# Attention keys in three chunks of 128 and a block-diagonal one, sums on VectorE and casts on ScalarE

## The chip, the cores and the metric

One core of a Trainium2 chip. The metric is the device time of one execution in microseconds (us). Engines: TensorE (PE; its weight loads are PEld), VectorE (DVE), ScalarE (ACT), GpSimd (POOL) and SyncE (SP), which issues all DMAs here. TensorE's clock has two levels, 1.2 and 2.4 GHz; the profile gives the granted one as a share of the higher.

## The reference

Attention with 4 batches, 12 heads, 448 positions and 64 columns a head, then two dense blocks on the 1792 x 768 result:

```python
scores = matmul(q, k.T) / 8
scores = cap * tanh(scores / cap)                # cap = 30
attn = softmax(scores)
x = matmul(attn, v)          # 1792 x 768 after the heads are joined
h = x @ w_in1;  x = (h - tanh(h)) @ w_out1       # 768 -> 2048 -> 768
h = x @ w_in2;  x = (h * sigmoid(1.702 * h)) @ w_out2
```

All weights come as 64-bit floats.

## The kernel before, in words

**Numbers.** Products are made from float32r parts: a value is cast to a high part, and a subtract gives the low part (`hi_act`, `hi_dve`, `lo_dve`, `lo_pool`, L92 to L102). A product of two split values takes three matmuls: high x high, low x high, high x low.

**Attention.** Heads go in pairs, six pairs a batch, 24 in all; q and k of two heads lie side by side in 128 partitions. The 448 keys of a head are four chunks of 112 (`C = 4`, `CP = 112`). For each pair:

- `load_qk` (four DMAs) and `load_v` (one) fetch it; `prep` transposes q and k on TensorE, casts the high part on ScalarE and subtracts on VectorE, 896 columns each; `v_split` does the same for v.
- `qk` makes the scores of one chunk, transposed: 112 keys x 448 queries of both heads. The two heads use the upper and the lower half of TensorE's rows, so six matmuls run as three pairs.
- `softmax` does tanh and a shifted exponential on ScalarE (112 x 896), the high cast `ph` and the low subtract `pl` on VectorE, and adds the exponentials to the running sum `s` on GpSimd (L312). No maximum is taken.
- `pv` multiplies the chunk with v: per head two matmuls, whose output holds the product with v's high part in one half of the partitions and with its low part in the other.
- `split_sum` splits the sum on VectorE; `pair_out` sums over partitions with a matrix of ones (four matmuls), takes the reciprocal on VectorE, joins the two halves and multiplies.

**Order.** `attention` is a generator written out by hand: it walks over the chunks with scores two chunks ahead of `pv` (`PV_LAG = 2`) and yields after each step, nine times a pair. Batch 0's attention runs alone until its last pair is out (L557). From then on a loop (L571) walks through the matrix work of a batch matmul by matmul and takes a step of the next batch's attention whenever `ATT_RATES` says that one is owed; no step falls due in the first quarter of batch 0. The tile framework then orders each engine's instructions statically, by program order and by what it reckons to be ready, and sets the waits; an engine runs its list in that order.

**Matrix work.** Per batch four parts (`gemm_in`, `gemm_out`, twice) of 288 matmuls of 448 columns. Weights come in chunks, fetched and split two chunks ahead (`ahead`). In batch 0 each is converted from its 64-bit form (`w_convert`, ScalarE and VectorE), split with the low part on GpSimd, and kept in DRAM; later batches read it back.

**Buffers.** Exponentials `t_p` three, high and low probabilities `ph_p` three each (the sum's parts among them), two PSUM tiles `ps_b` for scores, transposes, sums and output, a third one while batch 0's attention runs, one for `pv`.

Of the kernel before, what the change touches and what calls it, by code (L numbers as in the profile page):

```python
# [34 lines left out]
PV_LAG = 2  # L35

# [8 lines left out]
def attention_moe_moe(ctx, tc, q, k, v, cap, w_in1, w_out1, w_in2, w_out2, out):  # L45
# [11 lines left out]

    nc = tc.nc
# [3 lines left out]
    C = 4  # L62
    CP = S // C
# [10 lines left out]
    raw_p = pool("raw", 2)  # L74
    rv_p = pool("rawv", 1)
# [33 lines left out]
    ones = const.tile([CP, 2, P], F32R, name="ones")  # L109
# [10 lines left out]
    first = ExitStack()  # L120
    vs_f = first.enter_context(tc.tile_pool(name="vs_f", bufs=1))
# [123 lines left out]
    def load_v(g):
        if g >= NG:
            return
        b, hp = divmod(g, NP)
        tv = rv_p.tile([CP, 2, C, D], F32, tag="rv", name="rv")
        nc.sync.dma_start(  # L250
            out=tv.rearrange("p h c d -> p h (c d)"),
            in_=v[b, 2 * hp:2 * hp + 2].rearrange("h (p c) d -> p h (c d)", c=C),
        )
        rawv[g] = tv

    def prep(g):
        t = raw.pop(g)
        ps = big_ps(g, "ps_qk")
        for i in range(2):
            for c in range(C):  # L260
                nc.tensor.transpose(
                    ps[:, i, c * CP:(c + 1) * CP], t[:, i, c, :], ident[:CP, :CP]
                )
        h = qk_p.tile([P, 2, S], F32R, tag="qkh", name="qkh")
        l = qk_p.tile([P, 2, S], F32R, tag="qkl", name="qkl")
        hi_act(h, ps[:, :, :S])
        lo_dve(l, ps[:, :, :S], h)
        qkt[g] = (h, l)

    def v_split(g):  # L270
        tv = rawv.pop(g)
        t = (vs_f if g < NP and g % 2 else vs_p).tile([CP, 2, C, P], F32R, tag="vs", name="vs")
        for j in range(2):
            hh, ll = t[:, j, :, j * D:(j + 1) * D], t[:, j, :, (1 - j) * D:(2 - j) * D]
            hi_act(hh, tv[:, j])
            lo_dve(ll, tv[:, j], hh)
# [4 lines left out]
    def qk(n):  # L281
        g, c = divmod(n, C)
        h, l = qkt[g]
        ps = big_ps(g, "ps_sc")
        for m, (kk, qq) in enumerate(((h, h), (l, h), (h, l))):
            for j in range(2):
                a = slice(j * D, (j + 1) * D)
                nc.tensor.matmul(  # L288
                    ps[:CP, j, :S], kk[a, 1, c * CP:(c + 1) * CP], qq[a, 0, :], start=(m == 0), stop=(m == 2)
                )  # L290
        sc_ps[n] = ps

    def softmax(n):
        g, c = divmod(n, C)
        ps = sc_ps.pop(n)
        t = t_p.tile([CP, 2, S], F32, tag="t", name="t")
        nc.scalar.activation(out=t, in_=ps[:CP, :, :S], func=AF.Tanh, scale=tsc[:CP])  # L297
        nc.scalar.activation(out=t, in_=t, func=AF.Exp, scale=cpos[:CP], bias=cshift[:CP])  # L298
        h = ph_p.tile([CP, 2, S], F32R, tag="ph", name="ph")
        l = ph_p.tile([CP, 2, S], F32R, tag="pl", name="pl")  # L300
        hi_dve(h, t)
        lo_dve(l, t, h)
        phl[n] = (h, l)
        if c == 0:
            pt[g] = t
            return
        if c == 1:
            sums[g] = s_p.tile([CP, 2, S], F32, tag="s", name="s")
            a = pt.pop(g)
        else:  # L310
            a = sums[g]
        nc.gpsimd.tensor_tensor(out=sums[g], in0=a, in1=t, op=ALU.add)  # L312

    def pv(n):
        g, c = divmod(n, C)
        h, l = phl.pop(n)
        if c == 0:
            pvs[g] = ps_v.tile([P, 2, 512], F32, tag="v", name="ps_pv")
        for j in range(2):
            for m, pp in enumerate((h, l)):  # L320
                nc.tensor.matmul(  # L321
                    pvs[g][:, j, :S], vsp[g][:, j, c, :], pp[:, j, :],
                    start=(c == 0 and m == 0), stop=(c == C - 1 and m == 1),
                )

    def split_sum(g):
        s = sums.pop(g)
        h = ph_p.tile([CP, 2, S], F32R, tag="ph", name="sh")
        l = ph_p.tile([CP, 2, S], F32R, tag="pl", name="sl")
        hi_dve(h, s)  # L330
# [290 lines left out]
```

## Time and profile before

| | us |
|---|---|
| median of 3 runs (lowest, highest) | 1409.39 (1408.37, 1414.51) |
| profiled execution | 1408.85 |
| its span, first to last instruction | 1406.8 |
| busy: TensorE, VectorE, ScalarE, GpSimd | 1253.5, 1087.6, 822.2, 506.9 |

Batch 0's attention alone lasts until 150.7 us of the span, batch 0's matrix work until 555.5, batch 1's until 869, batch 2's until 1164.5. Busy time of TensorE is modelled from pipelined matmuls, so the distance from start to start is the better price of one.

### The profile page before, as it was taken

To read this page: it belongs to the slowest core of one execution; us is meant where nothing else is said; L and a number is where in the kernel's file an instruction comes from. 1 tells how busy PE (TensorE), PEld (TensorE's weight loads), DVE (VectorE), ACT (ScalarE), POOL (GpSimd) and SP (SyncE) were. 2 spreads that over 40 slices of the span, in tenths; PEclk is the share of its full clock that TensorE was granted. 3 is DMA by queue.
4 is the path that set the end of the run, shared out by engine and by line. 5 is a ranking of instruction groups with operands and counts; after the bars stand their busy time and mean duration, and the time that the engine had idled before them with its cause. 6 is when DMAs were issued, how large, how long until landed. Compare 5 with 4: busy or idle time off the path is not lost.

```text
span 1406.8 us, 17148 instructions
## 1 busy us (share of the span) xinstructions
PE 1253.5 (89%) x5964; PEld 1060.2 (75%) x5964; DVE 1087.6 (77%) x1229; ACT 822.2 (58%) x1100; POOL 506.9 (36%) x274
## 2 busy tenths in 40 slices
PE   7677766887887869988999999999999999999998
PEld 3344655776666757776888788888888899999997
DVE  5999899898989988997677875997788766933432
ACT  5764687777776674874455544684455535733421
POOL 2444555655766453432124320431154212301300
PEclk6565999998898989999999999999999999999999
DMA  6233155777566655763323446734333347533332
GB/s 172 67 89 105 54 168 161 240 235 231 185 202 189 196 173 185 264 209 86 116 86 118 123 113 178 196 104 122 119 95 105 99 133 226 149 119 113 108 113 66
DMA packets 164550, 204.36 MB, mean 145 GB/s; under 512 B 53360, under 2 KB 121456, under 8 KB 164464
## 3 DMA queue, kind: packets, MB, share of 16 engines
q1 hardware_dynamic: 164464, 203.27, 47.6%
q8 instruction: 47, 0.77, 0.2%
q14 instruction: 39, 0.32, 0.1%
HBM read 157.45 MB, written 45.78 MB: 144 GB/s over the span
## 4 chain that ended last, share of the span: by engine, by line
PE 50%; DVE 8%; issue 3%; DMA 1%; ACT 1%; POOL 0%; SPq 0%; DVEq 0%; ACTq 0%; POOLq 0%
PE ps_y L486 26%; PE ps_h L466 18%; PE ps_pv L321 3%; PE ps_sc L288 2%; DVE wl L99 1%; DVE r L347 1%; DVE g_q L439 1%; DVE g_t L437 1%; DMA wr<-kept 1%; PE ps_o L509 1%; DVE pl L99 1%; DVE g_q L440 1%; DVE ph L96 1%; PE ps_sum L339 0%; DVE g_far L426 0%
## 5 line engine op out<-in xcount | busy, mean ns | idle before, releaser
L466 PE MATMUL ps_h<-xh,wh 128*128 128x448 f32 x768 | 290.5, 379 | 46.5 <-DVE g_far L426 31.7
L486 PE MATMUL ps_y<-gh,wh 128*128 128x448 f32 x768 | 288.1, 375 | 15.9 <-DVE gh L96 8.1
L99 DVE TENSOR_TENSOR wl<-wr,wh 128x768 fp32r<-128x768 f32 (+1 forms) x172 | 170.9, 996 | 160.9 <-ACT wh L93 67.2
L466 PE MATMUL ps_h<-xl,wh 128*128 128x448 f32 x768 | 287.7, 375 | 4.1 <-DVE xl L99 4.1
L93 ACT CAST wh<-wr 128x768 fp32r<-128x768 f32 (+1 forms) x195 | 153.3, 786 | 235.7 <-PE ps_y L486 156.2
L486 PE MATMUL ps_y<-gl,wh 128*128 128x448 f32 x768 | 289.2, 377 | 1.6 <-POOL gl L102 1.6
L466 PEld LDWEIGHTS ps_h<-xh,wh 128*128 128x128 f32 x768 | 147.9, 193 | 73.1 <-DVE g_far L426 40.6
L312 POOL TENSOR_TENSOR s<-s,t 112x896 f32<-112x896 f32 x48 | 123.6, 2575 | 190.6 <-ACT t L298 190.2
L486 PE MATMUL ps_y<-gh,wl 128*128 128x448 f32 x768 | 189.7, 375 | 0.0
L466 PE MATMUL ps_h<-xh,wl 128*128 128x448 f32 x768 | 184.4, 371 | 0.0
L102 POOL TENSOR_TENSOR wl<-wr,wh 128x768 fp32r<-128x768 f32 (+1 forms) x68 | 145.8, 2147 | 105.7 <-DVE wh L96 62.9
L486 PEld LDWEIGHTS ps_y<-gh,wh 128*128 128x128 f32 x768 | 147.4, 192 | 35.2 <-DVE gh L96 8.8
L466 PEld LDWEIGHTS ps_h<-xl,wh 128*128 128x128 f32 x768 | 147.9, 193 | 19.0 <-DVE xl L99 4.3
L102 POOL TENSOR_TENSOR gl<-g_q,gh 128x448 fp32r<-128x448 f32 x64 | 91.5, 1429 | 194.7 <-ACT gh L93 111.2
L486 PEld LDWEIGHTS ps_y<-gl,wh 128*128 128x128 f32 x768 | 147.3, 192 | 18.8 <-issue 4.1
L99 DVE TENSOR_TENSOR pl<-t,ph 112x896 fp32r<-112x896 f32 x96 | 157.9, 1644 | 2.1
L486 PEld LDWEIGHTS ps_y<-gh,wl 128*128 128x128 f32 x768 | 146.5, 192 | 16.8 <-issue 3.8
L466 PEld LDWEIGHTS ps_h<-xh,wl 128*128 128x128 f32 x768 | 145.2, 190 | 16.4 <-issue 4.2
L102 POOL TENSOR_TENSOR gl<-g_g,gh 128x448 fp32r<-128x448 f32 x64 | 92.0, 1439 | 175.2 <-ACT gh L93 115.3
L297 ACT ACTIVATE t<-ps_sc,tsc 112x896 f32<-112x896 f32 x96 | 96.4, 1006 | 84.5 <-PE ps_sc L288 77.8
L96 DVE CAST ph<-t 112x896 fp32r<-112x896 f32 x96 | 102.4, 1066 | 38.7 <-ACT t L298 26.8
L193 ACT ACTIVATE wd<-wd 128x768 uint16<-128x768 uint16 (+1 forms) x68 | 125.2, 1849 | 1.1
(73 smaller groups left out, 1868.8 us busy)
## 6 DMA issues: line engine op xcount, KB each, us to landing
wr<-kept SPq DMA_DIRECT2D x100, 384.0 KB, 3.1
wd<-in_moe_w_in_dram SPq DMA_DIRECT2D x64, 384.0 KB, 4.4
wr<-kept SPq DMA_DIRECT2D x72, 320.0 KB, 3.0
wd<-in_moe_w_out_dram SPq DMA_DIRECT2D x48, 384.0 KB, 4.2
kept<-wr SPq DMA_DIRECT2D x44, 384.0 KB, 5.0
wh<-kept_hl SPq DMA_DIRECT2D x32, 384.0 KB, 3.3
wl<-kept_hl SPq DMA_DIRECT2D x32, 384.0 KB, 3.8
kept<-wr SPq DMA_DIRECT2D x24, 320.0 KB, 4.9
```

The costliest lines, as they stand in the source:

```text
L93: nc.scalar.copy(out=dst, in_=src)
L96: nc.vector.tensor_copy(out=dst, in_=src)
L99: nc.vector.tensor_tensor(out=dst, in0=src, in1=hi.bitcast(F32), op=ALU.subtract)
L102: nc.gpsimd.tensor_tensor(out=dst, in0=src, in1=hi.bitcast(F32), op=ALU.subtract)
L193: nc.scalar.mul(out=half[:, :, :, 2], in_=half[:, :, :, 1], mul=F64_LOW)
L288: nc.tensor.matmul(ps[:CP, j, :S], kk[a, 1, c * CP:(c + 1) * CP], qq[a, 0, :], start=(m == 0), stop=(m == 2))
L297: nc.scalar.activation(out=t, in_=ps[:CP, :, :S], func=AF.Tanh, scale=tsc[:CP])
L312: nc.gpsimd.tensor_tensor(out=sums[g], in0=a, in1=t, op=ALU.add)
L321: nc.tensor.matmul(pvs[g][:, j, :S], vsp[g][:, j, c, :], pp[:, j, :], start=(c == 0 and m == 0), stop=(c == C - 1 and m == 1),)
L347: nc.vector.reciprocal(out=r, in_=ps[:, 0, :S])
L466: nc.tensor.matmul(ps[:, :S], w[:, kk, :], x[kk], start=(m == 0), stop=(m == len(seq) - 1))
L486: nc.tensor.matmul(ps[:, :S], w[:, f - f0, :], x[f], start=(c == 0 and m == 0), stop=(c == len(parts) - 1 and m == len(seq) - 1),)
```

## The change

Keys become three chunks of 128 (`C = 3`) and a rest of 64 keys a head (`T = 64`). The rests of the two heads share one chunk of 128 partitions: k's is laid out block-diagonally, zero elsewhere, and v's rest has zeros in the other head's partitions. So a pair has three chunks of 128 x 896 and one of 128 x 448, whose scores are three matmuls over all 128 rows. The zeros are set once, in fixed tiles for q, k and v, two of each (one for v after batch 0).

The high casts of the exponentials and of the sum go to ScalarE, the running sum to VectorE; it leaves the last chunk out, whose exponentials go straight into the matmuls with ones (six instead of four, with a third block of ones). q and k are cast and subtracted separately; v's cast and subtract are one instruction each. The reciprocal takes a buffer of `t_p`. The steps are written out: seven a pair. q and k of a pair are eight DMAs, v's four, the output's two.

```diff
-                last_raw[0] = nc.sync.dma_start(
-                    out=t[:, i, :, j * D:(j + 1) * D], in_=src[b, 2 * hp + j].rearrange("(p c) d -> p c d", c=C)
+                e = slice(j * D, (j + 1) * D)
+                h = src[b, 2 * hp + j]
+                nc.sync.dma_start(
+                    out=t[:, i, :C, e], in_=h[:C * P].rearrange("(p c) d -> p c d", c=C)
                 )
+                a = j * T * i
+                last_raw[0] = nc.sync.dma_start(out=t[a:a + T, i, C, e], in_=h[C * P:])
...
+            for c in range(C + 1):
+                n = P if c < C or i else T
+                nc.tensor.transpose(ps[:, i, c * P:c * P + n], t[:n, i, c, :], ident[:n, :n])
+        h = qk_p.tile([P, S + SK], F32R, tag="qkh", name="qkh")
+        l = qk_p.tile([P, S + SK], F32R, tag="qkl", name="qkl")
+        for a, z, x in ((0, S, ps[:, 0, :S]), (S, S + SK, ps[:, 1, :SK])):
+            hi_act(h[:, a:z], x)
+            lo_dve(l[:, a:z], x, h[:, a:z])
...
+        t = (vs_f if g < NP and g % 2 else vs_p).tile([P, 2, C + 1, P], F32R, tag="vs", name="vs")
+        hi_act(t[:, :, :, :D], tv)
+        lo_dve(t[:, :, :, D:], tv, t[:, :, :, :D])
...
-    def qk(n):
-        g, c = divmod(n, C)
+    def qk(g, c):
         h, l = qkt[g]
         ps = big_ps(g, "ps_sc")
+        k0 = S + c * P
         for m, (kk, qq) in enumerate(((h, h), (l, h), (h, l))):
+            if c == C:
+                nc.tensor.matmul(ps[:, 0, :S], kk[:, k0:k0 + P], qq[:, :S], start=(m == 0), stop=(m == 2))
+                continue
             for j in range(2):
                 a = slice(j * D, (j + 1) * D)
-                nc.tensor.matmul(
-                    ps[:CP, j, :S], kk[a, 1, c * CP:(c + 1) * CP], qq[a, 0, :], start=(m == 0), stop=(m == 2)
-                )
-        sc_ps[n] = ps
...
+                nc.tensor.matmul(ps[:, j, :S], kk[a, k0:k0 + P], qq[a, :S], start=(m == 0), stop=(m == 2))
...
-        hi_dve(h, t)
...
+        hi_act(h, t)
         lo_dve(l, t, h)
...
-        nc.gpsimd.tensor_tensor(out=sums[g], in0=a, in1=t, op=ALU.add)
...
+        elif c < C:
+            a = pt.pop(g) if c == 1 else sums[g]
+            if c == 1:
+                sums[g] = s_p.tile([P, 2, S], F32, tag="s", name="s")
+            nc.vector.tensor_tensor(out=sums[g], in0=a, in1=t, op=ALU.add)
...
-                    pvs[g][:, j, :S], vsp[g][:, j, c, :], pp[:, j, :],
-                    start=(c == 0 and m == 0), stop=(c == C - 1 and m == 1),
+                    pvs[g][:, j, :S], vsp[g][:, j, c, :], pp[:, j if c < C else 0, :],
+                    start=(c == 0 and m == 0), stop=(c == C and m == 1),
...
+        if c < C:
+            phl.pop((g, c))
...
-        hi_dve(h, s)
+        h = ph_p.tile([P, 2, S], F32R, tag="ph", name="sh")
+        l = ph_p.tile([P, 2, S], F32R, tag="pl", name="sl")
+        hi_act(h, s)
         lo_dve(l, s, h)
...
+        th, tl = phl.pop((g, C))
...
-        for m, (j, pp) in enumerate(((0, h), (0, l), (1, h), (1, l))):
-            nc.tensor.matmul(ps[:, 0, :S], ones[:, j, :], pp[:, j, :], start=(m == 0), stop=(m == 3))
+        seq = [(2, th[:, 0]), (2, tl[:, 0])] + [(j, pp[:, j]) for j in range(2) for pp in (h, l)]
+        for m, (j, pp) in enumerate(seq):
+            nc.tensor.matmul(ps[:, 0, :S], ones[:, j, :], pp, start=(m == 0), stop=(m == len(seq) - 1))
...
-        r = s_p.tile([P, S], F32, tag="r", name="r")
+        r = t_p.tile([P, S], F32, tag="t", name="r")
...
-        load_qk(0)
-        load_qk(1)
-        load_v(0)
         yield False
         prep(0)
         v_split(0)
+        load_qk(2)
         load_v(1)
         yield False
...
+        for g in range(NG + 1):
+            last = g > 0 and g % NP == 0
             if g < NG:
-                qk(n)
+                qk(g, 0)
+                qk(g, 1)
                 yield False
-                softmax(n)
-                if c == 0:
-                    load_qk(g + 2)
-                if c == 2 and g + 1 < NG:
-                    prep(g + 1)
-                    yield False
...
+                softmax(g, 0)
+            if g > 0:
+                pv(g - 1, 2)
+                split_sum(g - 1)
+                yield False
+                pv(g - 1, 3)
+                pair_out(g - 1)
+                yield last
+                if g >= NP and g < NG:
+                    v_split(g)
+                    load_v(g + 1)
+            if g == NG:
+                break
+            softmax(g, 1)
+            qk(g, 3)
+            qk(g, 2)
+            yield False
+            softmax(g, 3)
+            pv(g, 0)
+            yield False
+            softmax(g, 2)
+            if g + 1 < NG:
+                prep(g + 1)
+                load_qk(g + 3)
+                yield False
+                if g + 1 < NP:
                     v_split(g + 1)
                     load_v(g + 2)
...
+            pv(g, 1)
+            yield False
...
+        nc.tensor.transpose(ps[:T, C * P:], y[:, C * P:], ident)
+        nc.vector.tensor_copy(out=o[:, :C].rearrange("p c e -> p (c e)"), in_=ps[:, :C * P])
+        nc.scalar.copy(out=o[:T, C], in_=ps[:T, C * P:])
+        dst = out[b * S:(b + 1) * S, e * P:(e + 1) * P]
+        nc.sync.dma_start(out=dst[:C * P].rearrange("(p c) e -> p c e", c=C), in_=o[:, :C])
+        nc.sync.dma_start(out=dst[C * P:], in_=o[:T, C])
...
+    for t in raws_qk:
+        nc.vector.memset(t[:, 1, C], 0.0)
+    for t in raws_v:
+        nc.vector.memset(t[:, :, C], 0.0)
+    load_qk(0)
     nc.sync.dma_start(out=capr, in_=cap.partition_broadcast(P))
+    load_v(0)
+    load_qk(1)
...
-    per_batch = 9 * NP
+    per_batch = 7 * NP
```

## Rows read from the trace of the kernel before

**Rows 1.** Windows: start:end, length, busy us (instructions) by engine, granted clock, DMA share, GB/s
```profile
12.00:150.70 138.70, 95.40 (x331) 57.35 (x329) 125.90 (x125) 92.12 (x105) 60.83 (x24) 0.62 0.36 100
150.70:244.40 93.70, 67.55 (x293) 57.43 (x293) 89.64 (x102) 70.34 (x98) 49.05 (x28) 0.95 0.44 136
244.40:327.50 83.10, 74.02 (x342) 64.33 (x343) 73.55 (x80) 62.41 (x65) 46.32 (x23) 0.94 0.70 228
327.50:430.00 102.50, 82.88 (x370) 69.44 (x369) 90.27 (x90) 77.70 (x86) 68.65 (x35) 0.88 0.66 212
430.00:555.50 125.50, 100.29 (x477) 82.89 (x478) 112.83 (x112) 79.68 (x90) 62.32 (x29) 0.88 0.58 183
555.50:869.00 313.50, 295.46 (x1473) 252.74 (x1472) 248.19 (x287) 174.73 (x257) 89.75 (x50) 0.99 0.46 140
869.00:1164.50 295.50, 291.49 (x1477) 253.57 (x1476) 226.72 (x262) 160.85 (x239) 89.92 (x49) 1.00 0.44 128
```

**Rows 2.** Lines by shape, whole span: busy us, mean ns; idle before it and releaser
```profile
L99 DVE TENSOR_TENSOR pl<-t,ph 112x896 fp32r<-112x896 f32 x96 | 157.9, 1644 | 2.1
...
L312 POOL TENSOR_TENSOR s<-s,t 112x896 f32<-112x896 f32 x48 | 123.6, 2575 | 190.6 <-ACT t L298 190.2
L298 ACT ACTIVATE t<-t,cshift,cpos 112x896 f32<-112x896 f32 x96 | 108.6, 1133 | 1.5
...
L96 DVE CAST ph<-t 112x896 fp32r<-112x896 f32 x96 | 102.4, 1066 | 38.7 <-ACT t L298 26.8 <-PE ps_pv L321 11.1
...
L297 ACT ACTIVATE t<-ps_sc,tsc 112x896 f32<-112x896 f32 x96 | 96.4, 1006 | 84.5 <-PE ps_sc L288 77.8 <-issue 6.5
L93 ACT CAST wh<-wr 128x768 fp32r<-128x768 f32 x111 | 92.3, 832 | 117.7 <-PE ps_y L486 55.5 <-PE ps_h L466 42.4 <-DVE wr L195 12.1
...
L99 DVE TENSOR_TENSOR sl<-s,sh 112x896 fp32r<-112x896 f32 x24 | 26.0, 1084 | 0.8
...
L93 ACT CAST gh<-g_g 128x448 fp32r<-128x448 f32 x32 | 18.2, 569 | 39.0 <-DVE g_g L457 39.0
...
L99 DVE TENSOR_TENSOR xl<-xs,xh 128x448 fp32r<-128x448 f32 x24 | 15.1, 632 | 3.6 <-ACT xh L93 3.6
```

**Rows 3.** Instructions of the tile ph: shortest, median and longest ns, first and last start
```profile
L96 DVE CAST ph<-t x96: 600/627/4293, 18.8 to 1134.6; 112x896 fp32r<-112x896 f32 x96
L99 DVE TENSOR_TENSOR pl<-t,ph x96: 1020/1093/3016, 19.4 to 1135.3; 112x896 fp32r<-112x896 f32 x96
```

**Rows 4.** Timelines of GpSimd and VectorE: start, us; an add and a low subtract
```profile
83.11 2.33 POOL L312 TENSOR_TENSOR s<-t 112x896 f32<-112x896 f32 x1 [3.19 <-DVE sl L99]
...
83.93 2.46 DVE L99 TENSOR_TENSOR pl<-t,ph 112x896 fp32r<-112x896 f32 x1
```

**Rows 5.** Timeline of VectorE: start, us; first and last of batch 0's six reciprocals
```profile
40.74 2.94 DVE L347 RECIPROCAL r<-ps_sum 128x448 f32<-128x448 f32 x1
...
147.69 2.94 DVE L347 RECIPROCAL r<-ps_sum 128x448 f32<-128x448 f32 x1
```

**Rows 6.** Timeline of TensorE: two matmuls at the half level; a score group, two at full
```profile
91.24 0.57 PE L321 MATMUL ps_pv<-ph,vs 112*128 112x448 f32 x1
91.61 0.57 PE L321 MATMUL ps_pv<-pl,vs 112*128 112x448 f32 x1
...
958.75 0.46 PE L288 MATMUL ps_sc<-qkh 64*112 64x448 f32 x2
...
959.55 0.89 PE L486 MATMUL ps_y<-gh,wl 128*128 128x448 f32 x3
...
963.31 0.36 PE L321 MATMUL ps_pv<-ph,vs 112*128 112x448 f32 x1
963.51 0.37 PE L321 MATMUL ps_pv<-pl,vs 112*128 112x448 f32 x1
```

**Rows 7.** SyncE's queue: a timeline row of two issues; a row of its waits (us, times, longest)
```profile
1.18 1.38 SPq L240 DMA_DIRECT2D raw<-in_q_dram  x2
...
SPq L240 <- PE ps_qk L261: 28.9, 7, 7.0
```

More of the change, by code (lines that the diff above doesn't have):

```diff
@@ L33 @@
 ATT_END_0, ATT_END = 1.0, 0.97
-PV_LAG = 2
 EXP_TOP = 60.0
@@ L61, in attention_moe_moe @@
     P = 128
-    C = 4
-    CP = S // C
+    C = 3
+    T = S - C * P
+    SK = C * P + 2 * T
     NP = H // 2
@@ L108, in attention_moe_moe @@
     cshift = const.tile([P, 1], F32, name="cshift")
-    ones = const.tile([CP, 2, P], F32R, name="ones")
+    ones = const.tile([P, 3, P], F32R, name="ones")
+    raws_qk = [const.tile([P, 2, C + 1, 2 * D], F32, name=f"raw{i}") for i in range(2)]
+    raws_v = [const.tile([P, 2, C + 1, D], F32, name="rv0")]
     tsc = const.tile([P, 1], F32, name="tsc")
@@ L120, in attention_moe_moe @@
     first = ExitStack()
+    rv_f = first.enter_context(tc.tile_pool(name="rv_f", bufs=1))
+    raws_v.append(rv_f.tile([P, 2, C + 1, D], F32, name="rv1"))
     vs_f = first.enter_context(tc.tile_pool(name="vs_f", bufs=1))
@@ L248, in load_v @@
         b, hp = divmod(g, NP)
[L249 to L252, printed above, removed]
-        )
+        tv = raws_v[g % 2 if g < NP else 0]
+        for j in range(2):
+            h = v[b, 2 * hp + j]
+            nc.sync.dma_start(
+                out=tv[:, j, :C].rearrange("p c d -> p (c d)"), in_=h[:C * P].rearrange("(p c) d -> p (c d)", c=C)
+            )
+            nc.sync.dma_start(out=tv[j * T:(j + 1) * T, j, C], in_=h[C * P:])
         rawv[g] = tv
@@ L271, in v_split @@
         tv = rawv.pop(g)
[L272 to L276, printed above, removed]
+        t = (vs_f if g < NP and g % 2 else vs_p).tile([P, 2, C + 1, P], F32R, tag="vs", name="vs")
+        hi_act(t[:, :, :, :D], tv)
+        lo_dve(t[:, :, :, D:], tv, t[:, :, :, :D])
@@ L302, in softmax @@
+        sc_ps[g, c] = ps
+    def softmax(g, c):
+        ps = sc_ps.pop((g, c))
+        n = 1 if c == C else 2
+        t = t_p.tile([P, n, S], F32, tag="t", name="t")
+        nc.scalar.activation(out=t, in_=ps[:, :n, :S], func=AF.Tanh, scale=tsc)
+        nc.scalar.activation(out=t, in_=t, func=AF.Exp, scale=cpos, bias=cshift)
+        h = ph_p.tile([P, n, S], F32R, tag="ph", name="ph")
+        l = ph_p.tile([P, n, S], F32R, tag="pl", name="pl")
+        hi_act(h, t)
         lo_dve(l, t, h)
-        phl[n] = (h, l)
+        phl[g, c] = (h, l)
@@ L317, in pv @@
+    def pv(g, c):
+        h, l = phl[g, c]
         if c == 0:
@@ L545, in attention_moe_moe @@
     nc.vector.tensor_scalar(out=cshift, in0=cshift, scalar1=0.0, scalar2=None, op0=ALU.min)
-    for j in range(2):
-        nc.vector.tensor_scalar(
-            out=ones[:, j, j * D:(j + 1) * D], in0=ident[:CP, :D], scalar1=0.0, scalar2=1.0,
-            op0=ALU.mult, op1=ALU.add,
-        )
-        nc.vector.tensor_scalar(
-            out=ones[:, j, (1 - j) * D:(2 - j) * D], in0=ident[:CP, :D], scalar1=0.0, scalar2=None, op0=ALU.mult
-        )
+    for m in range(3):
+        for j in range(2):
+            a = slice(j * D, (j + 1) * D)
+            for z in range(2):
+                nc.vector.tensor_scalar(
+                    out=ones[z * T:(z + 1) * T, m, a], in0=ident[z * T:(z + 1) * T, :D], scalar1=0.0,
+                    scalar2=float(j == (z if m == 2 else m)), op0=ALU.mult, op1=ALU.add,
+                )
     nc.vector.reciprocal(out=tsc, in_=cpos)
```

60 lines of the change are left out of this document (6 added, 54 removed).

## The prediction

> **What bounds the kernel now.** I read the stages first, by the busy time of each engine in eight stretches of the span [rows 1]; the reader is to see which engine is nearly full in each. From 12 to 150.7 us attention of batch 0 runs alone: VectorE is busy 125.9 of 138.7 us, ScalarE 92.1, TensorE 95.4 at a mean granted clock of 0.62. The four stretches from 150.7 to 555.5 are batch 0's matrix work, the conversion of the weights and attention of batch 1: VectorE is again fullest, 89.6 of 93.7, then 73.6 of 83.1 (TensorE 74.0 there), 90.3 of 102.5, 112.8 of 125.5. From 555.5 on TensorE is the bound: 295.5 of 313.5, then 291.5 of 295.5 at full clock. So 543 us hang mostly on VectorE, and 851 on TensorE.
>
> Next, the groups of instructions by shape [rows 2], and the shortest and median instance of two of them [rows 3]. The high cast of a chunk's exponentials (ph) has a mean of 1066 ns but a median of 627 and a longest of 4293; the low subtract (pl) 1644 against 1093 and 3016. GpSimd's own adds last 2575 ns. One add runs from 83.11 to 85.44; a low subtract that starts at 83.93 ends at 86.39, 0.95 us after it [rows 4]. So VectorE does not only do the work, it waits behind GpSimd, and those waits count as busy.
>
> The Trainium skill, SBUF — State Buffer, section "SBUF: two separate sides", says that the port pair of VectorE and GpSimd is an exclusive lock: a VectorE instruction in a two-port mode, or with two SBUF inputs, is blocked for the whole of a GpSimd instruction that reads SBUF. The excess in the rows agrees in kind. By the rule alone, three adds a pair could cost up to 3 x 2.58 = 7.7 us of VectorE per pair; the rows' excess, (1066 - 627) x 4 + (1644 - 1093) x 4, is 4.0 us, and I use that.
>
> Then the reciprocals, one per pair: the first of batch 0 starts at 40.74 and the sixth at 147.69, so a pair takes 107/5 = 21.4 us there [rows 5]. Last TensorE's order of time [rows 6]: a single attention matmul takes 0.20 us at the full level and 0.37 at the half level (1.2 GHz); six score matmuls, run as three pairs, take 959.55 - 958.75 = 0.80 us, of which 3 x 0.20 is streaming and 0.20 is going from whole-height to half-height use and back.
>
> **VectorE, per pair.** Before: four ph, four pl, the sum's cast and its subtract: 4 x 1.066 + 4 x 1.644 + 0.63 (as a ph median) + 1.084 = 12.6 us. After: three full subtracts, one half one (as a 448-column subtract, 0.632), the sum's subtract and two adds, each as sl, which no GpSimd add disturbs: 3 x 1.084 + 0.63 + 1.084 + 2 x 1.084 = 7.1 us [rows 2]. The low part of q and k becomes two instructions of 448 and 512 columns for one of 896, about +0.25. The saving is 5.2 us a pair, 31 over six. Were every new subtract as slow as pl's mean, 6.6 instances would cost 0.56 more each and it would be 1.5. Under the attention that runs alone GpSimd has almost nothing left, so I take 5.2; under batch 0 GpSimd still has the weights' low parts, but there the instances were slower too, and I take 5.
>
> **ScalarE, per pair.** Tanh and exponential fall from 4 x (1.006 + 1.133) = 8.6 us to three full ones and a half: 6.4 + about 1.3 (by 0.82 ns a column, below) = 7.7. New are the casts. A cast of 128x768 takes 0.832 and one of 128x448 0.569 us, so 0.82 ns a column and 0.94 us for 896 columns; bounds 0.83 and the 1.13 of an exponential of that size [rows 2]. Three full, one half, one of the sum: 4 x 0.94 + 0.57 = 4.3. The split cast of q and k adds 0.2, the joined cast of v gives that back. Net +3.5 us a pair (3.0 to 4.3), 21 us per batch. ScalarE had 46 us idle in the first stretch and 115 in batch 0, so this is hidden where VectorE set the end, unless its turn comes late.
>
> **TensorE, per pair.** Before: four score groups 3.2, sixteen probability matmuls 3.3, four sum matmuls 0.8: 7.3 us. After: chunks 0 and 1 as one group of twelve 1.4, chunk 2 0.8, the block-diagonal chunk three whole-height matmuls 0.6, sixteen probability matmuls 3.3, six sum matmuls 1.2: again 7.3. Two matmuls more are paid by two fewer changes of height. Zero, with bounds -0.4 (both extra matmuls hidden in waits) and +0.4.
>
> The Trainium skill, TensorEngine Tiling (Array Packing), section "Tiling Modes", says that changing the tiling mode drains the engine. That is the 0.20 of the row; taking it as nothing, the sum would be +0.4 us a pair on TensorE, 5 us over the two batches that TensorE bounds.
>
> **The first stretch, followed through one pair at the half clock.** ScalarE does tanh, exponential and cast of chunk 0 to 3.1 us and of chunk 1 to 6.2, with the sum's cast in a hole between. TensorE meanwhile does the last score groups, eight probability matmuls and six sum matmuls (14 x 0.37 = 5.2, plus 2 of scores): done at about 7.2. The reciprocal takes 2.94 [rows 5], the two adds and the multiply 3 x 0.6: 12.0. The reciprocal now takes one of three buffers of the exponentials, so chunk 3's tanh waits for that multiply; q's and k's casts and a weight conversion fill ScalarE until then. Chunk 1's subtract and add end at 14.2 and free the next buffer. Chunks 3 and 2 take ScalarE from about 12.6 to 17.6, and the next pair's chunk 0 follows. A pair takes about 17.5 us for 21.4, and what is late next is ScalarE behind that chain. Over five intervals and the tail: -20 us. At the head, the q and k of the first pair are eight issues instead of four; two issues take 1.38 us on the queue [rows 7], so four more are 2.8 us later, less where the first scores were late anyway: +2. The first weight loads now queue behind the third pair's q and k, which wait for the first transposes; their conversions have the whole stretch to be done in, so nothing.
>
> **Batch 0's matrix work.** No attention is due in its first quarter: nothing. In the last three stretches six pairs take 5 us each off VectorE, 30 of 277 us, and ScalarE rises by 21 from 220 of 311. VectorE stood at 89 per cent of these stretches, so of 30 I take nine tenths: -27, some -17 of it in the last one, where TensorE's 100.3 becomes the next floor under 125.5. Bounds: 0, if weights and GpSimd set the pace, and -40, if the slow instances all go.
>
> **Batches 1 and 2.** TensorE's sum is unchanged. In batch 1 it idles 18 us, the first quarter being VectorE's: -5 of it. In batch 2 it idles 4 us: a gain can be no more than 4, and I put +1 for the new waits below. Batch 3 has no attention: 0. Its last output leaves by two DMAs and two copies, side by side on two engines: 0.
>
> **Waits added.** (a) The high cast now needs ScalarE to find a free probability buffer of three, one of which the last chunk holds until the sum's matmuls of the next step. Behind a cast that waits stand ScalarE's weight casts and the matrix work's tanh, and for these TensorE waits. No row shows it; bounds 0 and, by the longest stall of ph (4293 - 627), 3.7 us a pair; I take 0.2 where TensorE is the bound, since each has steps of matmuls between. (b) The q and k loads move from a pair earlier to right behind the transposes that empty their buffer. Seven such waits cost the load queue 28.9 us [rows 7], about 4 each, and the weight loads queue behind; weights are fetched two chunks ahead, 36 matmuls or 7 us, so I take nothing; without that cover it would be 18 x 4 = 72 us. (c) A pair issues twelve loads instead of five, 7 x 0.69 = 4.8 us of queue time; hidden, as the queue mostly waits.
>
> **Sum.** 1408.85 (the profiled execution, span 1406.8 and 2 us around it; the median is 1409.39, so the two agree) - 20 + 2 - 27 - 5 + 1 = 1360 us.
>
> **Rivals.** *ScalarE takes VectorE's place* (0.18). For it: ScalarE's queue is in order, its work in the first stretch becomes 92 + 21 = 113 of then 119 us, nearly as full as VectorE was, and a cast waits where an add on GpSimd waited for nobody. Against: 161 us of idle before 555.5. Then a pair takes 20 us in the first stretch (-7 + 2) and batch 0 gives a third (-9): 1395.
>
> *More than the sum* (0.17). TensorE's granted clock is 0.62 in the first stretch, between its two levels, with the engine 69 per cent busy; closer work could hold 2.4 GHz, and the walk's 7.2 us becomes about 4. Then 15 us a pair (-32) and batch 0 gives its bound of -40: 1332.
>
> *The new waits reach TensorE* (0.11). One mechanism: the scarce probability buffer in (a). At 3.7 us for each of the 18 pairs that run beside matrix work it costs 67, and 1360 + 67 = 1427, slower than before. It decides from 49/18 = 2.7 us a pair. Against: TensorE hardly waits for attention in batch 2 now, and each pair there has 49 us.
>
> *The lock stays* (0.04). GpSimd keeps the weights' and the activations' low parts, so in batch 0 VectorE may be blocked as often: its saving is then 1.5 us a pair and batch 0 gives 8: 1379.
>
> **How the numbers follow.** 0.50 for the sum's case, 1345 to 1378. The range, 1328 to 1402, leaves out the slower rival and the ends. Half a per cent, 7 us, is what a measurement can tell from no change. Faster: 0.50 + 0.17 + 0.04, and 0.13 of the first rival: 0.84. Same: its remaining 0.05 and 0.01 of the slower one: 0.06. Slower: 0.10.
>
> **What would show it.** Right: reciprocals of batch 0 17 to 18 us apart; low subtracts near 1.09 mean; ScalarE, not VectorE, fullest before 150 us; casts of 896 columns near 0.94; the stretch before the second batch ends some 45 us earlier; batch 2 unchanged within 3 us. Wrong: reciprocals still 20 or more apart with ScalarE waiting inside the pair; TensorE waiting for ScalarE's casts in batches 1 and 2; VectorE's subtracts as long as before.

## The result, and the profile after

The changed kernel takes 1373.99 us (median of 4 runs, 1372.21 to 1375.37) against 1408.88 for the one before; ratio 0.9744, 95% interval 0.9715 to 0.9772. It is faster by 35 us. The forecast was 1360, its range 1328 to 1402. The profiled execution took 1372.21 us, its span 1370.4.

Cut at the first matmul of each batch's matrix work, the two spans compare like this (us; before, these matmuls start at 150.7, 552.5, 868.7 and 1163.0, after at 149.0, 528.2, 834.4 and 1127.7):

| stage | before | after | difference | predicted |
|---|---|---|---|---|
| first stretch | 150.7 | 149.0 | -1.7 | -20 +2 |
| batch 0 | 401.8 | 379.2 | -22.6 | -27 |
| batch 1 | 316.2 | 306.2 | -10.0 | -5 |
| batch 2 | 294.3 | 293.3 | -1.0 | +1 |
| batch 3 | 243.8 | 242.7 | -1.1 | 0 |

So three of the five terms came out near what was put down, and the first stretch gave almost nothing. The windows of the kernel after, in the columns of [rows 1] and cut at the corresponding places:

```profile
12.00:149.00 137.00, 93.71 (x332) 59.36 (x332) 96.93 (x107) 107.76 (x133) 5.40 (x3) 0.71 0.37 107
149.00:242.50 93.50, 71.45 (x302) 61.57 (x300) 89.25 (x102) 74.15 (x103) 49.04 (x27) 0.89 0.44 140
242.50:323.00 80.50, 72.85 (x336) 62.89 (x337) 72.69 (x78) 66.96 (x72) 38.10 (x21) 0.94 0.75 237
323.00:415.00 92.00, 75.75 (x349) 64.53 (x348) 75.46 (x80) 74.18 (x83) 49.91 (x29) 0.93 0.69 215
415.00:528.20 113.20, 100.02 (x484) 83.87 (x485) 96.18 (x106) 93.03 (x116) 39.10 (x21) 0.94 0.65 207
528.20:834.40 306.20, 296.65 (x1483) 260.11 (x1482) 219.07 (x270) 200.21 (x298) 47.03 (x32) 0.99 0.48 148
834.40:1127.70 293.30, 291.12 (x1465) 258.85 (x1464) 199.78 (x247) 180.18 (x271) 43.53 (x32) 0.99 0.44 127
```

The first line is the one to look at. VectorE fell from 125.9 busy us [rows 1] to 96.9, ScalarE rose from 92.1 to 107.8, GpSimd has 5.4 left, and yet the stretch is as long as before: no engine is full in it. ScalarE stands idle 29 of 137 us, VectorE 40, TensorE 43. That is the picture of a chain through several engines, not of a full one. In batch 0 VectorE's work did leave: 363.3 us busy from 150.7 to 552.5 before, 333.6 from 149.0 to 528.2 after.

The groups by shape, in the columns of [rows 2], price the moved operations:

```profile
L99 DVE TENSOR_TENSOR pl<-t,ph 128x896 fp32r<-128x896 f32 x72 | 87.3, 1213 | 41.7 <-ACT ph L93 41.5
...
L93 ACT CAST ph<-t 128x896 fp32r<-128x896 f32 x72 | 67.9, 945 | 2.6 <-PE ps_pv L327 1.7
...
L319 DVE TENSOR_TENSOR s<-s,t 128x896 f32<-128x896 f32 x24 | 33.3, 1387 | 6.8 <-ACT t L307 6.8
L99 DVE TENSOR_TENSOR sl<-s,sh 128x896 fp32r<-128x896 f32 x24 | 30.7, 1280 | 14.6 <-ACT sh L93 14.6
L319 DVE TENSOR_TENSOR s<-t 128x896 f32<-128x896 f32 x24 | 28.6, 1193 | 6.8 <-ACT t L307 6.6
...
L93 ACT CAST qkh<-ps_qk 128x512 fp32r<-128x512 f32 x24 | 14.0, 584 | 16.9 <-DVE qkl L99 16.9
```

The cast of 896 columns takes 0.945 us, as estimated. The low subtract fell from 1644 ns [rows 2] to 1213, not to the 1.084 taken, and VectorE now waits 41.5 us before it for ScalarE's casts, where it waited 2.1 in all. By stretch the subtract takes 1.086 us while attention runs alone, 1.487 in batch 0, 1.188 and 1.087 in batches 1 and 2: most of the excess lies in batch 0, where GpSimd is busy 176 of 379 us (more on this at the end).

The first and the last of batch 0's six reciprocals, as in [rows 5], on VectorE's timeline:

```profile
44.65 2.96 DVE L357 RECIPROCAL r<-ps_sum 128x448 f32<-128x448 f32 x1 [0.21 <-PE ps_sum L349]
...
145.66 2.96 DVE L357 RECIPROCAL r<-ps_sum 128x448 f32<-128x448 f32 x1
```

They stand 101.0/5 = 20.2 us apart, where 17.5 was predicted and 21.4 was before; the first comes 3.9 us later. The waits of the first stretch (12 to 149 us; engine and line that waits, what for, us, times, longest):

```profile
...
DVE pl L99 <- ACT ph L93: 21.9, 9, 5.1
PEld ps_sc L299 <- ACT qkh L93: 20.4, 7, 5.3
PE ps_sc L299 <- ACT qkh L93: 17.6, 7, 5.1
ACT t L306 <- PE ps_sc L299: 12.4, 5, 4.1
```

TensorE's scores wait for ScalarE's cast of q and k, ScalarE's tanh for those scores, VectorE's subtracts for ScalarE. One pair of ScalarE's timeline shows the order (start, us, ... the idle before it in brackets):

```profile
111.55 0.63 ACT L306 ACTIVATE t<-ps_sc,tsc 128x448 f32<-128x448 f32 x1 [1.88 <-DVE s L319]
112.08 0.52 ACT L93 CAST qkh<-ps_qk 128x448 fp32r<-128x448 f32 x1
...
112.96 0.77 ACT L307 ACTIVATE t<-t,cshift,cpos 128x448 f32<-128x448 f32 x1
113.62 1.00 ACT L306 ACTIVATE t<-ps_sc,tsc 128x896 f32<-128x896 f32 x1
114.51 0.56 ACT L93 CAST ph<-t 128x448 fp32r<-128x448 f32 x1
114.97 1.14 ACT L307 ACTIVATE t<-t,cshift,cpos 128x896 f32<-128x896 f32 x1
116.00 0.58 ACT L93 CAST qkh<-ps_qk 128x512 fp32r<-128x512 f32 x1
...
119.51 1.01 ACT L306 ACTIVATE t<-ps_sc,tsc 128x896 f32<-128x896 f32 x1 [2.09 <-PE ps_sc L299]
...
122.57 0.93 ACT L93 CAST sh<-s 128x896 fp32r<-128x896 f32 x1
```

The pair's last two chunks start at 111.55, when the first add has freed a buffer: it stood behind the reciprocal on VectorE (107.37 to 110.33). k's cast (128x512) stands behind their exponentials and comes at 116.00, the next pair's scores follow at 116.64, tanh can go on only at 119.51, the sum's cast comes at 122.57 and the next reciprocal at 125.99. The walk had q's and k's casts in the hole before 111.55, and it had chunk 3's tanh wait for the multiply, where it waits for the first add.

For k's cast there was no place in that hole, whatever the order on ScalarE: in all 24 pairs it starts only after q's low subtract on VectorE has ended, and all of its 16.9 us of waits are for that subtract (the last row of the groups above). In this pair the subtract stands behind the reciprocal on VectorE's timeline:

```profile
112.91 0.62 DVE L99 TENSOR_TENSOR qkl<-ps_qk,qkh 128x448 fp32r<-128x448 f32 x1
```

It ends at 113.53, 2.0 us after the hole. The kernel before has one cast for q and k, and no such wait.

### The profile page after: what moved, and what is told of

The parts are those of the page before. It is cut to its first block, busy times and chain, and to the rows that moved or that the text cites. A ratio compares the mean times of both kernels' runs of the same rounds, so it can differ in the third digit from the quotient of the medians.

```text
span 1370.4 us, 17486 instructions
## 1 busy us (share of the span) xinstructions
PE 1245.2 (91%) x5940; PEld 1072.5 (78%) x5940; DVE 970.1 (71%) x1169; ACT 902.4 (66%) x1244; POOL 311.9 (23%) x202
## 4 chain that ended last, share of the span: by engine, by line
PE 51%; DVE 7%; ACT 3%; issue 2%; DMA 1%; POOL 0%; DVEq 0%; ACTq 0%; SPq 0%
PE ps_y L504 26%; PE ps_h L484 18%; PE ps_pv L327 2%; PE ps_sc L299 2%; DVE g_q L457 2%; DVE g_t L455 1%; DVE g_q L458 1%; PE ps_sum L349 1%; PE ps_qk L272 1%; DVE g_far L444 1%; DVE wl L99 1%; PE ps_o L528 0%; DVE r L357 0%; PE ps_sc L295 0%; ACT g_v L451 0%
## 5 line engine op out<-in xcount | busy, mean ns | idle before, releaser
L99 DVE TENSOR_TENSOR wl<-wr,wh 128x768 fp32r<-128x768 f32 (+1 forms) x172 | 164.0, 955 | 178.5 <-PE ps_y L504 87.1
L102 POOL TENSOR_TENSOR wl<-wr,wh 128x768 fp32r<-128x768 f32 (+1 forms) x68 | 135.5, 1995 | 294.7 <-ACT ph L93 102.1
L504 PE MATMUL ps_y<-gh,wl 128*128 128x448 f32 x768 | 186.5, 371 | 0.0
L102 POOL TENSOR_TENSOR gl<-g_g,gh 128x448 fp32r<-128x448 f32 x64 | 86.4, 1351 | 363.0 <-ACT gh L93 280.0
L484 PEld LDWEIGHTS ps_h<-xh,wl 128*128 128x128 f32 x768 | 146.4, 191 | 14.5 <-issue 1.2
L99 DVE TENSOR_TENSOR pl<-t,ph 128x896 fp32r<-128x896 f32 (+1 forms) x96 | 105.0, 1096 | 49.5 <-ACT ph L93 49.3
L306 ACT ACTIVATE t<-ps_sc,tsc 128x896 f32<-128x896 f32 (+1 forms) x96 | 87.6, 913 | 42.3 <-PE ps_sc L299 20.1
L307 ACT ACTIVATE t<-t,cshift,cpos 128x896 f32<-128x896 f32 (+1 forms) x96 | 99.8, 1042 | 1.7
L199 DVE SCALAR_TENSOR_TENSOR wr<-wd,wr 128x768 uint32<-128x768 uint32 (+1 forms) x68 | 81.0, 1192 | 16.7 <-ACT wd L197 12.4
```

The costliest lines, as they stand in the source:

```text
L99: nc.vector.tensor_tensor(out=dst, in0=src, in1=hi.bitcast(F32), op=ALU.subtract)
L102: nc.gpsimd.tensor_tensor(out=dst, in0=src, in1=hi.bitcast(F32), op=ALU.subtract)
L199: nc.vector.scalar_tensor_tensor(out=u, in0=high, scalar=0x80000007, in1=u, op0=ALU.bitwise_and, op1=ALU.bitwise_or)
L306: nc.scalar.activation(out=t, in_=ps[:, :n, :S], func=AF.Tanh, scale=tsc)
L307: nc.scalar.activation(out=t, in_=t, func=AF.Exp, scale=cpos, bias=cshift)
L484: nc.tensor.matmul(ps[:, :S], w[:, kk, :], x[kk], start=(m == 0), stop=(m == len(seq) - 1))
```

## The experiments

All are compared in the first stretch by its length, and by the starts of its six reciprocals. Times are medians. Stage lengths are read from one traced execution of each kernel, and executions of one kernel lie 1 to 8 us apart, so a few us in a late stage prove little.

**The reciprocal in a buffer of its own** during the first stretch, so that it doesn't hold one of the three of the exponentials:

```diff
-        r = t_p.tile([P, S], F32, tag="t", name="r")
+        r = (
+            rec_f.tile([P, S], F32, tag="rec", name="r") if g < NP else t_p.tile([P, S], F32, tag="t", name="r")
+        )
```

> The changed kernel (1374 us), with one edit: while batch 0's attention runs alone, the reciprocal has a buffer of its own and takes none of the three buffers of the exponentials. Theory buffers: in the changed kernel chunk 3's tanh waits 1.9 to 3.1 us a pair for the first add of the sum, which itself stands behind the reciprocal on VectorE; with a free buffer it goes right behind chunk 1's cast, so reciprocals stand 16.5 to 17.5 us apart where they stood 18.6 to 19.7 without weight conversions, the first stretch ends 8 to 11 us earlier, total 1363 to 1367. Rival full engine: ScalarE is simply full (107.8 of 137 us and in order), the wait moves to the next pair's first tanh; total within 3 us of 1374. Later stretches unchanged under both.

Measured 1359.12, ratio 0.9641 (0.9616 to 0.9666): 15 us below the changed kernel, 4 below the range named. The first stretch takes 141.0, 8.0 less, as the theory had it, but the reciprocals stand 18.8 apart, not 16.5 to 17.5; most of the rest lies in batch 1 (5.0 us), where neither side had a gain. The buffer is part of the chain, but not all of it.

**q and k of the next pair ahead of chunk 2's softmax** (`prep`, `load_qk`), all else as changed:

```diff
-            softmax(g, 2)
             if g + 1 < NG:
                 prep(g + 1)
                 load_qk(g + 3)
                 yield False
+            softmax(g, 2)
```

> The changed kernel with one edit: in the written-out order the transposes and casts of the next pair's q and k stand ahead of chunk 2's tanh instead of behind its cast. Theory late keys: k's high cast comes one exponential earlier (1.1 us), so the next pair's first scores and its tanh, which waits 2.1 us a pair, come up to 1.1 us earlier; six pairs in the first stretch, 4 to 7 us, total 1367 to 1371. Rival full engine: the earlier cast only pushes chunk 2's exponential back by its own 0.6 us and nothing is gained: within 3 us of 1374.

Measured 1349.24, ratio 0.9568 (0.955 to 0.9586): 25 us below the changed kernel, more than either side expected. The first stretch ends at 130.8, 18.2 sooner; 9.1 of that come before the first reciprocal and 8.8 between the first and the sixth. Batches 0 and 1 give 7 more (376.2 and 302.0 us), which nobody had named. The reciprocals of the third to sixth pair stand 16.6 to 17.0 apart. ScalarE's timeline in it:

```profile
98.25 0.63 ACT L306 ACTIVATE t<-ps_sc,tsc 128x448 f32<-128x448 f32 x1 [1.88 <-DVE s L319]
...
101.67 0.60 ACT L93 CAST qkh<-ps_qk 128x512 fp32r<-128x512 f32 x1
102.14 1.16 ACT L307 ACTIVATE t<-t,cshift,cpos 128x896 f32<-128x896 f32 x1
103.33 0.94 ACT L93 CAST ph<-t 128x896 fp32r<-128x896 f32 x1
104.26 1.01 ACT L306 ACTIVATE t<-ps_sc,tsc 128x896 f32<-128x896 f32 x1
```

k's cast now stands ahead of chunk 2's exponential, 3.4 us behind the pair's chunk 3 where it was 4.5, and the next tanh (104.26) waits for nothing: the 2.09 us are gone. The wait of 1.88 for the add is still there. The edit moves the transposes, q's cast and the loads along with k's cast; the run with k's cast alone stands below. At the head the first reciprocal starts at 35.53 instead of 44.65: the second pair's k cast comes at 23.46, ahead of the first weight conversions, where in the changed kernel it stands behind two of them, one of which waits for its load:

```profile
29.20 0.89 ACT L196 ACTIVATE wr<-wd 128x768 f32<-128x768 f32 x1 [1.86 <-DMA wd<-in_moe_w_in_dram]
29.99 0.56 ACT L93 CAST qkh<-ps_qk 128x512 fp32r<-128x512 f32 x1
```

That pair's chunk 0 follows at 35.14, and the cast of the first pair's sum stands behind it in ScalarE's list, at 39.41.

**Both together:**

> Both edits of the two runs before (own buffer for the reciprocal in the first stretch, q and k of the next pair ahead of chunk 2's tanh). Theory buffers and late keys: the two waits lie in the same chain one behind the other, so the gains add: reciprocals 15.5 to 16.5 us apart, 12 to 18 us off the first stretch, total 1356 to 1363. Rival full engine: ScalarE has about 15.5 us of work a pair, so no more than 4 us is gained: 1370 to 1375.

Measured 1363.26, ratio 0.9658 (0.9641 to 0.9674): a miss, 14 us slower than the earlier q and k alone. With the buffer free, the framework puts chunk 1's tanh ahead of chunk 0's cast in ScalarE's list:

```profile
107.45 0.54 ACT L93 CAST qkh<-ps_qk 128x448 fp32r<-128x448 f32 x1 [2.26 <-PE ps_qk L273]
...
113.59 1.01 ACT L307 ACTIVATE t<-ps_sc,tsc 128x896 f32<-128x896 f32 x1 [1.75 <-PE ps_sc L300]
114.63 1.13 ACT L308 ACTIVATE t<-t,cshift,cpos 128x896 f32<-128x896 f32 x1
115.67 0.99 ACT L307 ACTIVATE t<-ps_sc,tsc 128x896 f32<-128x896 f32 x1
116.56 0.93 ACT L93 CAST ph<-t 128x896 fp32r<-128x896 f32 x1
117.39 0.94 ACT L93 CAST sh<-s 128x896 fp32r<-128x896 f32 x1
```

The tanh at 115.67 holds up the two casts behind it, on which the sum and so the reciprocal wait. The transposes also come late here: q's cast waits 2.26 us for them, k's (110.43) stands behind chunk 2's exponential again, and the next tanh waits 1.75 us for its scores. The inner pairs take 18.2 us; the two gains don't add. Most of the loss, though, lies in the first two intervals (28.0 and 22.0 us, for 23.2 and 18.8 with the earlier q and k alone), and no run takes those apart.

**Only the keys' high cast to VectorE**, in the order of the changed kernel:

```diff
-            hi_act(h[:, a:z], x)
+            (hi_dve if a else hi_act)(h[:, a:z], x)
```

> The changed kernel with the keys' high cast alone moved from ScalarE to VectorE. Theory (the scores of the next pair come late because the keys' cast stands in ScalarE's row behind the weight conversions and the exponentials of chunks 3 and 2): first reciprocal at 36 to 40 where it was 44.65, reciprocals nearer than 20.2, time 1350 to 1364. Rival (VectorE's row is as late there, behind the reciprocal and the sum's additions, and the keys' cast only changes place in the chain): within 3 us of 1374.

Measured 1366.99, ratio 0.9672 (0.9656 to 0.9688): 7 us below the changed kernel, 3 above the range named. VectorE's timeline, second to fifth reciprocal:

```profile
71.75 2.96 DVE L357 RECIPROCAL r<-ps_sum 128x448 f32<-128x448 f32 x1 [0.41 <-PE ps_sum L349]
88.78 2.96 DVE L357 RECIPROCAL r<-ps_sum 128x448 f32<-128x448 f32 x1
105.80 2.96 DVE L357 RECIPROCAL r<-ps_sum 128x448 f32<-128x448 f32 x1
122.81 2.96 DVE L357 RECIPROCAL r<-ps_sum 128x448 f32<-128x448 f32 x1
```

These are 17.0 us apart, three times over, where the same four of the changed kernel stand 22.5, 19.5 and 18.6 apart. So a second edit, of one line, shows that in these pairs k's cast on ScalarE is what cost the time. At the head the expectation failed: the first reciprocal comes at 47.68, 24.1 ahead of the second. There ScalarE's list has weight conversions of 1.9 us ahead of the second pair's tanh and exponential as well:

```profile
32.93 1.91 ACT L197 ACTIVATE wd<-wd 128x768 uint16<-128x768 uint16 x1
...
35.43 0.99 ACT L306 ACTIVATE t<-ps_sc,tsc 128x896 f32<-128x896 f32 x1
36.32 1.90 ACT L197 ACTIVATE wd<-wd 128x768 uint16<-128x768 uint16 x1
```

The last pair takes 22.2 here; why, was not tried. With these two ends the first stretch is only 0.9 us shorter than in the changed kernel (148.1, in the trace of the slowest of four executions, 1372.34), so the 7 us of the median are not read from this trace.

**The sum's high cast to VectorE**, on top of the earlier q and k (`hi_dve` for `hi_act` in `split_sum`):

> The kernel with the next pair's queries and keys ahead of chunk 2 (1349), with the sum's high cast moved from ScalarE to VectorE. Theory (batch 0's first stretch is one chain, sum -> its cast -> its split -> sum matmuls -> reciprocal -> product, and the sum's cast stands on ScalarE behind chunk 0's exponential and cast): the split starts about 1 us sooner a pair, the reciprocals come 15 to 16 us apart where they were 16.65, time 1339 to 1347. Rival (ScalarE's own work per pair is already the bound of that stretch, or VectorE loses with the cast what it gains): reciprocals no closer than 16.5, time 1347 to 1354.

Measured 1352.77, ratio 0.9579 (0.9565 to 0.9594), the third to the fifth reciprocal 16.65 apart as without it, first stretch 131.4: no gain, the rival's case. The test is weaker than meant, since the cast found no free buffer (VectorE's timeline):

```profile
106.37 0.63 DVE L96 CAST sh<-s 128x896 fp32r<-128x896 f32 x1 [1.47 <-PE ps_pv L327]
```

**The engines alone, in the old chunks and the old order.** First the sums only, then the sums and both casts, each an edit of the kernel before:

```diff
-        nc.gpsimd.tensor_tensor(out=sums[g], in0=a, in1=t, op=ALU.add)
+        nc.vector.tensor_tensor(out=sums[g], in0=a, in1=t, op=ALU.add)
```

> The kernel before with one move alone: the three adds a pair on VectorE, casts still there, old chunks and order. Theory lock: 3.3 us of adds come on, 4.0 us of waits and more go, ScalarE gets nothing; casts near 0.65 and low subtracts near 1.15 us; total 1385 to 1400. Rival load: VectorE is what bounds the first 550 us, and adds on it cost what the waits give back: 1404 to 1415.

Measured 1374.46, ratio 0.9743 (0.9724 to 0.9762): the whole gain of the change, with one line, and 10 us below the range named. First stretch 135.7, batch 0 392.3. The casts fall from 1066 to 819 ns and the low subtracts from 1644 to 1189, so 2.8 of the 4.0 us a pair that the prediction read as waits behind GpSimd's adds are gone.

```diff
-        hi_dve(h, t)
+        hi_act(h, t)
...
-        hi_dve(h, s)
+        hi_act(h, s)
```

> The kernel before (1409 us) with the two engine moves alone: casts of the exponentials and of the sum on ScalarE, sums on VectorE; still four chunks of 112 and the old order of steps, with the transposes of the next pair between chunks 2 and 3. Theory: most of the gain in the matrix stretches is the moves', and the old order lacks the late keys of the new one, so the first stretch gains more than it did: total 1368 to 1385. Rival: the fewer columns and the fewer changes of TensorE's height carry the gain; then 1390 to 1405.

Measured 1356.51, ratio 0.961 (0.9594 to 0.9627), better than both sides expected: first stretch 136.9, batch 0 377.8. So the casts are worth another 18 us there, 14.5 of it in batch 0, and all the rest of the change (chunks, written-out order, the reciprocal's buffer, loads) costs 17.5 us, 12 of them in the first stretch. In the old order q and k stand behind the third of four chunks, ahead of the last one's softmax; the new order has them behind the last.

**The engines, undone one at a time in the changed kernel.** The sums back to GpSimd:

> The changed kernel (1374 us) with the running sum's adds on GpSimd again (two a pair), the casts still on ScalarE. Theory lock: the gain in batches 0 and 1 is that VectorE no longer waits behind GpSimd's adds; low subtracts of 896 columns go back from 1.2 to 1.4 us or more, the adds take 2.5 us in the chain that gates chunk 3's tanh, batch 0 is 6 to 12 us longer and the total 1384 to 1396. Rival: VectorE also loses two adds a pair (2.4 us), which outweighs a lock that only two adds a pair cause; total 1366 to 1374.

Measured 1377.48, ratio 0.9763 (0.9748 to 0.9779): between the two ranges named; the interval overlaps that of the changed kernel. Batch 0 is 6.0 us longer, the first stretch 4.0 shorter. Then both casts back to VectorE, first in the changed kernel, then in the one with q and k earlier:

> The changed kernel with one part undone: the high casts of the exponentials and of the sum are on VectorE again, the sums stay on VectorE. Theory lock: most of the gain in batch 0 and 1 comes from taking the adds off GpSimd, so the gain mostly stays: VectorE rises by some 2.8 us a pair and ScalarE falls by 4.3; total 1372 to 1385. Rival load: it comes from taking the casts off VectorE, which bounds batch 0; then 17 us of six pairs go back onto it: 1388 to 1398. In the first stretch, if ScalarE is what is full there now, this undoing makes that stretch shorter by 5 us or more.

Measured 1370.6, ratio 0.9717 (0.9703 to 0.9732): no slower than with the casts on ScalarE, and just below the theory's range. The first stretch takes 151.5, 2.5 more, so ScalarE's load did not set it. Batch 0's matrix work in one line each, for the kernel before, for the one with the sums alone moved, and for this one (columns as in [rows 1]):

```profile
150.70:552.50 401.80, 321.73 (x1466) 271.32 (x1467) 363.29 (x379) 289.20 (x334) 226.12 (x114) 0.91 0.59 189
135.70:527.90 392.20, 323.36 (x1465) 270.65 (x1466) 372.23 (x408) 294.04 (x338) 190.89 (x99) 0.92 0.64 205
151.50:531.50 380.00, 321.55 (x1467) 275.17 (x1466) 346.74 (x393) 287.58 (x345) 176.51 (x97) 0.92 0.63 198
```

The length does not follow VectorE's busy time: the second has 8.9 us more of it than the kernel before and is 9.6 shorter, and the third has 13.1 more than the changed kernel (333.6) and is 0.8 longer.

> The changed kernel with two edits: q and k of the next pair ahead of chunk 2's tanh (1349 us alone) and the casts back on VectorE (1371 alone). If the earlier keys' 25 us come from a chain through ScalarE, which is lighter here by 4.3 us a pair, the gain adds up: 1340 to 1350. Rival: with the casts on VectorE the first stretch is bound by VectorE again (reciprocals 20 or more apart), and the order of the keys gives little: 1362 to 1371.

Measured 1359.47, ratio 0.9643 (0.9616 to 0.967), between the two sides: 10 us slower than with the casts on ScalarE.

## Why the prediction was right or wrong, point by point

- **First stretch, -20 +2: wrong, -1.7 measured.** The failed step is "q's and k's casts and a weight conversion fill ScalarE until then". In the trace q's cast stands behind chunk 3's tanh, and k's behind both of the pair's last exponentials, because `prep` comes behind chunk 2's softmax in the new order. An engine runs its list in order, so the hole was waited out and the next pair's scores came 2.1 us late for ScalarE. The walk also lacked k's wait for q's low subtract, which keeps that cast out of the hole in any order on ScalarE. With `prep` one step earlier the stretch ends 19.9 us sooner than before; with k's cast on VectorE the inner pairs take 17.0 us. That the inner pairs come so near the walk's 17.5 is partly luck: with `prep` earlier, chunk 0's tanh to chunk 3's takes 10.6 us (104.26 to 114.90) where the walk has 12.6, and from there to the next pair's chunk 0 it takes 6.0 (98.25 to 104.26) where the walk has 5.0. Over all five intervals the two kernels stand at 18.4 and 19.5.
- **At the head, +2: +3.9, for another reason.** The loads of q and k cost nothing: the first tanh starts at 14.98 us, before at 15.82. The first weight loads, which the prediction put at nothing, are issued from 21.70 us instead of 7.25, and two conversions stand ahead of the second pair's k cast (29.99), one after a wait of 1.86 for its load. With q and k earlier the cast is ahead of them, and the first reciprocal comes 5.2 us sooner than before.
- **Batch 0, -27: near, -22.6, but its reason is not shown.** VectorE lost 29.7 busy us for 30 expected, ScalarE gained 19.1 (289.2 to 308.3) for 21. Yet the windows above say that VectorE's busy time does not set the length. GpSimd lost 50 us (226.1 to 176.2); whether its lighter list is what made the stretch shorter was not tried. The last of the four stretches gave 9.3 (122.5 to 113.2, cut at batch 1's first matmul) where -17 was put down; in it TensorE (100.0 of 113.2) is now the fullest, as the prediction had it.
- **Batch 1, -5: right in kind, -10.** TensorE's idle time there went from 18.0 us [rows 1] to 9.6, and of what is left 3.9 is one wait for a low part on GpSimd.
- **Batches 2 and 3: within 2.1 us, and TensorE's zero not contradicted.** Nine kernels with the new chunks have batch 2 at 291.7 to 294.1, the three with the old ones at 289.4 to 294.3; a difference of half a microsecond a pair could hide in that.
- **The waits added.** (a) For a free probability buffer ScalarE's casts of ph wait 2.6 us in all, 1.7 of it for TensorE, and the sum's 11.5; TensorE's waits in batch 2 are 1.9 us in all. Right. (b) and (c): SyncE waits 53.5 us for the transposes, 13 times; 47.5 of it are five waits in the first stretch, up to 15.4 long, where about 4 each were put down. From 149 us on no matmul waits for a load, as forecast.
- **The rivals.** "ScalarE takes VectorE's place" named 20 us a pair for the first stretch and that came, but with ScalarE idle for 29 us: its place in the order, not its load, set the end; casts back on VectorE don't help (21.3 us apart). Its -9 for batch 0 didn't come. "More than the sum" needed the full clock; the granted clock rose to 0.71 only (and the sum behind its 1332 leaves out the +2 and the +1; with them it is 1335). Nor does the clock sort the kernels: it is 0.73 in the 130.8 us of the one with `prep` earlier and 0.77 in the 151.5 us of the one with the casts on VectorE. The lock stayed in part, as that rival had it, in batch 0: there pl takes 1.49 for the 1.084 of the sum, the second add 2.14, while in the first stretch they take 1.09.
- **The total.** 1374 lies within the 1345 to 1378 of the sum's case, but that case did not hold: 16 us are missing in the first stretch and 4 in batch 0, and 8 came that were not put down in batches 1 to 3. Of the signs named, three came (ScalarE fullest in the first stretch, casts of 0.945, batch 2 unchanged) and three did not (reciprocals 17 to 18 us apart, subtracts of 1.09 in the mean, batch 0 ending 45 us earlier, where it was 24.3). One sign of being wrong came: reciprocals 20.2 apart with ScalarE waiting inside the pair.

What none of the steps saw is that the edits stand in for each other. Sums to VectorE: 36 us alone, some 3, within the noise, when undone in the changed kernel. Casts to ScalarE: 18 in the old order behind the sums, 10 with q and k early, nothing in the changed order. That the late keys are what hides these gains there is argued from the timelines, not shown; no run takes all of it apart. Open is also why the last pair is slow with k's cast on VectorE.

The best kernel here is the changed one with `prep` ahead of chunk 2's softmax: 1349.24 us.

## What to carry to other kernels

When a change rewrites the order of issue, read each engine's list from the code and walk through it with every cast and conversion in its place; a hole in an engine is filled only by what stands next in its list. Where no engine is full in a stretch, ask which short instruction of the next round stands behind the long ones of this round, and move that first: here one block of lines moved up was worth 25 us, two thirds of what the whole change gave. Splitting one instruction in two can also make one half wait for another engine, as k's cast did for q's subtract: ask for each new piece what it waits for. Test the parts of a change alone as well; the cheapest of them may carry it all.

## What the runs showed of the hardware

A VectorE subtract that meets an add on GpSimd is not slowed throughout but held up until the add ends. In the kernel with the sums on GpSimd (first GpSimd's timeline, then VectorE's):

```profile
99.33 2.10 POOL L319 TENSOR_TENSOR s<-s,t 128x896 f32<-128x896 f32 x1 [5.21 <-ACT t L307]
...
116.48 2.09 POOL L319 TENSOR_TENSOR s<-s,t 128x896 f32<-128x896 f32 x1 [4.89 <-ACT t L307]
```

```profile
100.53 1.84 DVE L99 TENSOR_TENSOR pl<-t,ph 128x896 fp32r<-128x896 f32 x1
104.79 1.09 DVE L99 TENSOR_TENSOR pl<-t,ph 128x896 fp32r<-128x896 f32 x1 [2.42 <-ACT ph L93]
...
117.68 1.84 DVE L99 TENSOR_TENSOR pl<-t,ph 128x896 fp32r<-128x896 f32 x1
```

Both adds end 0.9 us before the subtract that started under them, as in [rows 4]: the subtract waits for the add, then takes nearly its usual time. The Trainium skill, SBUF — State Buffer, section "SBUF: two separate sides", calls this an exclusive lock held for the whole instruction, and the rows agree. In the changed kernel's batch 0 the low parts that GpSimd makes do the same; of the 24 low subtracts and second adds of 896 columns there, the 10 that start under a GpSimd subtract take 2.01 to 2.75 us and end 0.95 us after it, and the other 14 take 1.08 to 1.09. One of each engine (GpSimd, VectorE):

```profile
283.80 1.66 POOL L102 TENSOR_TENSOR wl<-wr,wh 128x640 fp32r<-128x640 f32 x1 [1.45 <-DVE wh L96]
284.32 2.10 DVE L99 TENSOR_TENSOR pl<-t,ph 128x896 fp32r<-128x896 f32 x1 [0.29 <-ACT ph L93]
```

The price in the whole is not shown apart: with the sums on GpSimd, batch 0 has 12 of its adds, 27 us at 2.25 (the mean of their groups, 2345 and 2149 ns), and grew by 6.0, but in the same edit VectorE gave up 12 adds of its own.
